# Second item's queries turned by DMA transposes, last item's values loaded in two halves at two times

## The chip, the cores and the metric

The kernel runs on one core of a Trainium2 chip. The metric is the device time of one execution in microseconds (us). A core has five engines that work at the same time, each through its own instructions in order: TensorE (PE in the profile, with its weight loads as PEld), VectorE (DVE), ScalarE (ACT), GpSimd (POOL) and SyncE (SP). Data moves between memory and the core's own buffers by DMA: the transfers that POOL issues run through one software queue (q0 in the profile), those that SP issues through one hardware queue (q1). An engine waits for another, or for a DMA, by a semaphore, and whatever stands behind a waiting instruction on the same engine waits with it.

## What is computed

```python
# B=4 items, H=8 heads, S=768 tokens, D=64; 8 blocks of 96 tokens
P = sinkhorn(sort_net)                     # 5 rounds of exp and row/column division
k_sorted = einsum('bhij,bhjcd->bhicd', P, k_blocks)
v_sorted = einsum('bhij,bhjcd->bhicd', P, v_blocks)
attn = softmax(q_block @ k_sorted_block.T / 8)     # inside each block
x = (attn @ v_sorted_block)                # 3072 tokens x 512
h1 = x @ w1; h2 = x @ w2
out = maximum(h1, h2) @ w_out              # fp32, 3072 x 512
```

## The kernel before

**Stages.** The four batch items are numbered 0 to 3. For each item the kernel sorts keys (`sort_k`, three groups of 32 small matmuls, called KS here), sorts values (`sort_v*`, VS), makes scores and exponentials (`scores`, eight units SC[0] to SC[7], the exponential on ACT), multiplies by values (`values`, VA[0] to VA[7]: eight matmuls into `o_ps`, then on DVE a reciprocal `rs` and a scaled copy `x`), and transposes the result (`x_transposes`, TR[0] to TR[3], into `xT`). Then the dense part follows: `moe_h` makes `max(h1, h2)` as relu((w1-w2)x) plus w2 x, whose second half goes through a product `wc` of w2 and w_out (`w_product`); `moe_out` multiplies by w_out and `wc` and writes the rows out.

**Order.** The order of instructions is written by hand. The first item is the list `front`. After it a loop runs over the items: the dense work of item b is cut into units (for b=0: units 0 to 7 are empty, 8 to 11 are the four `w_product`, 12 to 23 are halves of `moe_out`; for the others units 0 to 7 are `moe_h` and 8 to 19 halves of `moe_out`), and behind unit n stand the steps of the attention of item b+1 that `first_tail`, `second_tail` and `third_tail` list under n. So TensorE always has dense work between the attention steps. An even and an odd `ti` of `moe_out` share one tile `out_ps`; its copy to `o` stands behind the second half of the odd one, that is behind units 15, 19 and 23 of the first item and 11, 15 and 19 of the later ones. A greedy rule (`pick`) shares such copies between ACT and DVE by estimated load.

**Buffers the change touches.** `v_raw` holds raw values of two items side by side: rows 64 to 127 for item 1 and rows 0 to 63 for item 2. `TURN[0]` to `TURN[3]` (`turn_v` on DVE, L250, 24 of 96 columns each, all rows) rearrange it into `v_dc`, whose strided columns are the weights of VS. A VS needs all four turns. Then item 3's values are loaded twice, into both row halves, so that `sort_v_halved` can work from both. When those are turned, `v_raw` is free again and takes item 3's raw keys (columns of TURN[0] and TURN[1]) and raw queries (columns of TURN[2] and TURN[3]). `q_raw` has one buffer; item 2's queries go into the space of `w2_sb`. `q_pair` has one buffer.

**Queries.** `q_transposes(b, half)` makes half of `qT`. For items 0 and 1 it is 24 TensorE transposes into `tq_ps` (L433) and a copy on DVE; for items 2 and 3 `pair_q` first puts the two heads of a pair side by side (`q_pair`, DVE, L407) and SP issues one DMA transpose per half (L419). SC[0], SC[1], SC[4] and SC[5] read half 0, the other four half 1.

**Loads.** POOL issues all loads, in program order: after the weights, item 1's keys, item 1's queries, four pieces of values (items 1 and 2), item 2's keys, item 2's queries; from `first_tail` the four pieces of item 3's values; from `second_tail` item 3's keys and queries.

Of the kernel before, what the change touches and what calls it, by code (L numbers as in the profile page):

```python
# [11 lines left out]
BF16 = mybir.dt.bfloat16  # L12
# [4 lines left out]
def kernel(  # L17
# [16 lines left out]
    nc = tc.nc  # L34
# [12 lines left out]
    R = S // 128  # L47
    PB = 128 // NB
    HP = H // 2
# [5 lines left out]
    const = ctx.enter_context(tc.tile_pool(name="const", bufs=1))  # L55
# [60 lines left out]
    q_raw, qT = {}, {}  # L116
# [15 lines left out]
    def load_q(b, by_pair=False):  # L132
        if b == 2:
            t = w2_sb.rearrange("p t f -> p (t f)")[:, 0 : H * R * D].rearrange(
                "p (h x) -> p h x", h=H
            )
        elif b == 3:
            t = v_raw[:, HB * D :].rearrange("p (h x) -> p h x", h=H)
        else:
            t = qpool.tile([128, H, R * D], BF16, tag="q_raw", name="q_raw", bufs=1)  # L140
        src = q[b].rearrange("h (p r) d -> p h (r d)", r=R)
        for hs in [slice(hp, H, HP) for hp in range(HP)] if by_pair else [slice(0, H)]:
            nc.gpsimd.dma_start(out=t[:, hs], in_=src[:, hs])
        q_raw[b] = t

    k_raw = {}
    v_raw = big.tile([128, BLK * D], BF16, tag="v_raw", name="v_raw")
    k_src = k.rearrange("b h (j ch c) d -> b (h j ch) (c d)", j=NB, ch=2)
    v_src = v.rearrange("b h (j c) d -> b (h j) (c d)", j=NB)
    NCH = 3  # L150

    def load_k(b):
        k_raw[b] = (
            kpool.tile([128, HB * D], BF16, tag="k_raw", name="k_raw")
            if b < 3
            else v_raw[:, 0 : HB * D]
        )
        n = HB * D // NCH
        for ci in range(NCH):
            nc.gpsimd.dma_start(  # L160
                out=k_raw[b][:, ci * n : (ci + 1) * n],
                in_=k_src[b, :, ci * n : (ci + 1) * n],
            )

    def load_v(b, pieces=2, which=None, half=None):
        r0 = (b % 2 if half is None else half) * 64
        n = BLK * D // pieces
        for m in range(pieces) if which is None else [which]:
            nc.gpsimd.dma_start(  # L169
                out=v_raw[r0 : r0 + 64, m * n : (m + 1) * n],  # L170
                in_=v_src[b, :, m * n : (m + 1) * n],
            )
# [30 lines left out]
    def selections(b, eng=nc.gpsimd):  # L203
# [8 lines left out]
        if b == 0:  # L212
# [185 lines left out]
    nc.vector.memset(v_sb[:, :, D : D + 1], 1.0)  # L398
    xT = big.tile([128, 2, 2, 2, 2, TCH], BF16, tag="xT", name="xT")

    q_pair = {}

    def pair_q(b, two):

        if two == 0:
            q_pair[b] = qpool.tile([128, HP, R, 2 * D], BF16, tag="q_pair", name="q_pair", bufs=1)
        nc.vector.tensor_copy(  # L407
            out=q_pair[b][:, :, :, two * D : (two + 1) * D],
            in_=q_raw[b][:, two * HP : (two + 1) * HP].rearrange("p h (r d) -> p h r d", r=R),
        )  # L410
        load["D"] += 900

    def q_transposes(b, half, eng=None):

        if half == 0:
            qT[b] = qpool.tile([128, HP, R, 128], BF16, tag="qT", name="qT")
        if b > 1:
            hps = slice(half * 2, half * 2 + 2)
            nc.sync.dma_start_transpose(  # L419
                out=qT[b][:, hps].rearrange("p h r c -> p (h r) c"),  # L420
                in_=q_pair[b][:, hps].rearrange("p h r d -> p (h r d)"),
            )
            return
        ps = ps_bf16("tq_ps")
        if b == 0 and half == 0:
            nc.tensor.matmul(
                ps[:, 0:128], fill[:, 0:128], ident, is_transpose=True, start=True, stop=True
            )
        for n in range(2 * R):
            hp, r = half * 2 + n // R, n % R  # L430
            c = slice(n * 128, (n + 1) * 128)
            for h2 in range(2):
                nc.tensor.matmul(  # L433
                    ps[h2 * 64 : h2 * 64 + 64, c],
                    q_raw[b][:, hp + 4 * h2, r * D : (r + 1) * D],
                    ident,
                    is_transpose=True,
                    start=True,
                    stop=True,
                )  # L440
# [326 lines left out]
    turn_v(first, "A", 36, 56)  # L767
    turn_v(first, "A", 56, 80)
    block_diagonals_first()
    seen = const.tile([128, 2, 2], BF16, tag="seen", name="seen")  # L770
# [19 lines left out]
    def front_step(step):  # L790

        eng = step[-1] if step[-1] in "AD" else None
        name = step[:-1] if eng else step
        kind = name.rstrip("0123456789ab")
        n = [int(x) for x in name if x.isdigit()]
        if kind == "F":
            fills[0] = 512
        elif kind == "k":
            sort_k(0, n[0], 640 if step == front[0] else 0, eng)
        elif kind == "v":  # L800
            sort_v(0, n[0], 0, eng)
        elif kind == "tq":
            q_transposes(0, n[0], eng)
        elif kind == "SC":
            scores(0, n[0], fills_due())
        elif kind == "VA":
            values(0, n[0], fills_due())
        elif kind == "tx":
            x_transposes(0, n[0], eng)
        elif kind == "tw":  # L810
            w2_transposes(n[0], eng)()
        elif kind == "diff":
            w_difference(n[0])
# [15 lines left out]
    load_w(wo_sb, moe_w_out)  # L829
    w_difference(0, nc.gpsimd)  # L830
    w_difference(1, nc.gpsimd)
    load_k(1)
    for step in front[1:-26]:
        front_step(step)

    load_q(1)
    for piece in range(2):
        for b in (1, 2):
            load_v(b, which=piece)
    load_k(2)  # L840

    for step in front[-26:]:
        front_step(step)
    load_q(2)
    load.update(A=600.0, D=300.0)

    def turn(rows, c0):
# [3 lines left out]
    def sorts_and_scores(b):  # L851
# [2 lines left out]

    SC, VA, TR, KS = sorts_and_scores(1)
    VS = [lambda t=t: sort_v_pair(2, t) for t in range(8)]
    TQ = [lambda half=half: q_transposes(1, half) for half in range(2)]
# [40 lines left out]
    SC, VA, TR, KS = sorts_and_scores(3)  # L898
    third_tail = {
        0: [lambda: q_transposes(3, 0), lambda: q_transposes(3, 1)],  # L900
        2: KS,
        5: SC[0:2],
        6: [VA[0]],
        7: [VA[1], TR[0]],
        8: SC[2:5],
        9: [VA[2]],
        10: [VA[3], TR[1]],
        11: [VA[4]],
        12: SC[5:8],
        13: [VA[5], TR[2]],  # L910
        14: [VA[6]],
        16: [VA[7], TR[3]],
    }
    tails = [first_tail, second_tail, third_tail, {}]
    for b in range(B):
# [52 lines left out]
```

The softmax here doesn't subtract the row's maximum and nothing guards it: scores larger than these inputs give would overflow.

## Time and profile before

| what | value |
|---|---|
| time, median of 13 runs | 166.41 us (166.02 to 167.34) |
| the profiled execution's own time | 167.34 us |
| its span, first to last instruction | 165.5 us |
| granted TensorE clock | 1.000 |
| instructions | 4561 |
| software queue q0: packets, MB written | 11040, 13.37 |
| hardware queue q1: packets, MB | 19200, 10.17 |
| end of the front (start of item 1's KS) | 39.09 us |
| start of item 1's dense part | 71.79 us |
| start of item 2's dense part | 104.83 us |
| start of item 3's dense part | 136.47 us |

The profile is one execution. Its times count from the span's start; the time of the run has 1.8 us more, which lie outside the span. The loads read fp32 and write bf16, so the bytes that the profile gives for q0 are half of those read. "Landing" is the time from a DMA's issue to its last byte.

### The profile page before, as it was taken

Reading aid. Unit: us, or ns where it says so; the run is one execution under the profiler, and the core shown is the slowest. Engines: PE = TensorE matmul, PEld = TensorE weight load, DVE = VectorE, ACT = ScalarE, POOL = GpSimd, SP = SyncE. Lnnn points to the kernel's source line nnn. Section 1 sums busy time; section 2 is a strip of 40 time slices with the busy share of each in tenths; the row PEclk is TensorE's granted clock in tenths of the full one; section 3 lists DMA queues with packets and bytes.
Section 4 is the critical chain, followed back from the end, with each engine's and each line's share of the span. In section 5 each row is a group of like instructions: output and inputs, shape, how many; then the busy total and the mean of one; then the engine's idle time right before and its main releaser. Section 6 shows DMA issues by size and latency. Waiting matters only on the chain.

```text
span 165.5 us, 4561 instructions
## 1 busy us (share of the span) xinstructions
PE 158.1 (96%) x2007; PEld 96.7 (58%) x2025; DVE 77.3 (47%) x170; ACT 82.3 (50%) x101; POOL 33.4 (20%) x61
## 2 busy tenths in 40 slices
PE   7999997999999999999999999999999999999992
PEld 7959775666545555557655554575655546554451
DVE  5868994766276473535278764250642420000011
ACT  3588775816339847046751353467447306642020
POOL 7957987231206000000014020000000000000000
DMA  3999999999999999679525999991025294000333
GB/s 53 197 204 194 162 193 205 209 205 220 210 202 204 218 223 161 178 84 224 115 12 103 181 191 215 196 228 28 0 52 174 50 163 142 0 0 0 131 127 127
DMA packets 30404, 23.90 MB, mean 144 GB/s; under 512 B 16752, under 2 KB 25200, under 8 KB 30384
## 3 DMA queue, kind: packets, MB, share of 16 engines
q0 software_dynamic: 11040, 13.37, 48.6%
q1 hardware_dynamic: 19200, 10.17, 27.9%
q8 instruction: 16, 0.26, 0.7%
q10 hardware_dynamic: 144, 0.07, 0.1%
q14 instruction: 4, 0.03, 0.0%
HBM read 26.75 MB, written 6.29 MB: 200 GB/s over the span
## 4 chain that ended last, share of the span: by engine, by line
PE 87%; DMA 6%; ACT 2%; POOL 2%; issue 1%; DVE 0%
PE out_ps L704 37%; PE h_ps L677 25%; PE fill_ps L82 6%; DMA w_sb<-in_moe_w_dram 6%; PE wc_ps L657 4%; PE o_ps L575 4%; PE k_ps L458 3%; PE s_ps L548 3%; ACT e L556 1%; POOL w_sb L189 1%; PE v_ps L523 1%; PE tq_ps L433 1%; PE tw_ps L638 1%; PE v_ps L500 1%; ACT kT L108 1%
## 5 line engine op out<-in xcount | busy, mean ns | idle before, releaser
L704 PE MATMUL out_ps<-wo_sb,g 128*128 128x512 bf16 (+2 forms) x187 | 46.0, 370 | 1.4 <-issue 1.0
L677 PE MATMUL h_ps<-xT,w_sb 128*128 128x384 bf16 x256 | 44.5, 326 | 0.0
L677 PEld LDWEIGHTS <-w_sb 128*128 128x128 bf16 x256 | 24.0, 98 | 15.5
L556 ACT ACTIVATE e<-s_ps 96x768 bf16<-96x768 f32 x32 | 24.0, 807 | 14.8 <-PE s_ps L548 14.8
L691 ACT ACTIVATE g<-h_ps 128x768 bf16<-128x768 f32 x27 | 21.7, 812 | 17.2 <-PE h_ps L677 17.1
L704 PEld LDWEIGHTS <-g 128*128 128x128 bf16 x200 | 17.1, 97 | 15.8
L704 PE MATMUL out_ps<-wc,xT 128*128 128x512 bf16 (+2 forms) x98 | 24.7, 370 | 0.1
L108 ACT COPY o<-out_ps 128x1024 f32<-128x1024 f32 x10 | 10.1, 1013 | 28.0 <-PE out_ps L704 25.2
L592 DVE TENSOR_TENSOR x<-o_ps,rs 96x512 bf16<-96x512 f32 x32 | 22.0, 686 | 1.1
L704 PEld LDWEIGHTS <-xT 128*128 128x128 bf16 x100 | 9.6, 97 | 11.2
L575 PEld LDWEIGHTS <-e 96*128 96x128 bf16 x256 | 11.7, 97 | 5.8 <-DVE v_sb L110 0.2
L586 DVE RECIPROCAL rs<-o_ps 96x8 f32<-96x8 f32 x32 | 6.4, 199 | 17.9 <-PE o_ps L575 17.9
L739 DVE COPY o<-out_ps 128x512 f32<-128x512 f32 (+1 forms) x2 | 1.2, 625 | 27.6 <-PE out_ps L704 27.6
L575 PE MATMUL o_ps<-v_sb,e 96*128 96x65 bf16 x256 | 12.7, 193 | 0.0
L110 DVE CAST kT<-k_ps 128x1024 bf16<-128x1024 f32 x6 | 7.2, 1222 | 9.5 <-PE k_ps L458 9.5
L110 DVE CAST v_sb<-v_ps 96x1024 bf16<-96x1024 f32 x7 | 8.5, 1218 | 5.1 <-PE v_ps L523 2.2
L160 POOL DMA_DIRECT2D v_raw<-in_k_dram x3 | 2.5, 838 | 35.1 <-DVE v_dc L250 31.4
L108 ACT CAST v_sb<-v_ps 96x1024 bf16<-96x1024 f32 x9 | 8.8, 1017 | 1.5 <-PE v_ps L500 0.8
L82 PEld LDWEIGHTS <-fill 128*128 128x128 bf16 x98 | 8.1, 130 | 1.5 <-DVE fill L73 1.2
L169 POOL DMA_DIRECT2D v_raw<-in_v_dram x11 | 6.3, 579 | 12.8 <-DMA v_raw<-in_v_dram 5.6
L82 PE MATMUL fill_ps<-fill 128*128 128x118 bf16 x92 | 7.8, 274 | 1.2 <-DVE fill L73 1.2
L693 DVE TENSOR_SCALAR g<-h_ps 128x768 bf16<-128x768 f32 x5 | 4.8, 957 | 8.7 <-PE h_ps L677 8.6
(97 smaller groups left out, 145.3 us busy)
## 6 DMA issues: line engine op xcount, KB each, us to landing
out_dram<-o SPq DMA_DIRECT2D x11, 512.0 KB, 3.0
v_raw<-in_v_dram POOLq DMA_DIRECT2D x8, 384.0 KB, 13.8
k_raw<-in_k_dram POOLq DMA_DIRECT2D x9, 256.0 KB, 11.0
w_sb<-in_moe_w_dram POOLq DMA_DIRECT2D x4, 256.0 KB, 5.9
w_sb<-in_moe_w_dram POOLq DMA_DIRECT2D x2, 512.0 KB, 10.3
wo_sb<-in_moe_w_out_dram POOLq DMA_DIRECT2D x2, 512.0 KB, 13.9
v_raw<-in_v_dram POOLq DMA_DIRECT2D x3, 256.0 KB, 4.6
q_raw<-in_q_dram POOLq DMA_DIRECT2D x4, 192.0 KB, 8.8
```

The lines of the kernel that those rows point to most:

```text
L82: nc.tensor.matmul(ps[:, 0:w], w0, fill[:, 0:w], start=True, stop=True)
L108: nc.scalar.copy(out=out_ap, in_=in_ap)
L110: nc.vector.tensor_copy(out=out_ap, in_=in_ap)
L169: nc.gpsimd.dma_start(out=v_raw[r0 : r0 + 64, m * n : (m + 1) * n], in_=v_src[b, :, m * n : (m + 1) * n],)
L556: nc.scalar.activation(out=e[:, 0 : 8 * BLK].rearrange("p (t c r) -> p t c r", t=8, r=R), in_=ps[0:BLK] .rearrange("p (t f) -> p t f", t=8 ...
L575: nc.tensor.matmul(ps[:, h2 * 512 + ii * 65 : h2 * 512 + (ii + 1) * 65], e[:, (h2 * 4 + ii) * BLK : (h2 * 4 + ii) * BLK + 128], v_sb[:, m0 ...
L586: nc.vector.reciprocal(out=rs, in_=ov[:, :, :, 64])
L592: nc.vector.tensor_tensor(out=x, in0=ov[:, :, :, 0:D], in1=rs.to_broadcast([BLK, 2, 4, D]), op=ALU.mult,)
L657: nc.tensor.matmul(ps[:, 0:512], w2T[:, fb, dmt * 128 : (dmt + 1) * 128], wo_sb[:, fb, :], start=(fb == 0), stop=(fb == NFB - 1),)
L677: nc.tensor.matmul(h_ps[ch, t][:, m * 512 : m * 512 + TCH], w1_sb[:, hp, fb * 128 : (fb + 1) * 128], xT[:, b % 2, ch, hp % 2, hp // 2, :], ...
L691: nc.scalar.activation(out=g, in_=src, func=AF.Relu)
L704: nc.tensor.matmul(dst, g_tiles[b, ch, m // 2][:, m % 2, off : off + 128] if m < NFB else xT[:, b % 2, ch, hp % 2, hp // 2, off : off + 12 ...
```

## The change

Item 1's queries are transposed by DMA, as items 2 and 3 are. Their load moves ahead of the keys'. A new `hold_loads` puts a POOL copy of four bytes out of `qT` in front of the following loads: POOL waits there until that half of `qT` is complete. The values of items 1 and 2 are loaded in eight pieces behind this hold, then item 2's queries, then its keys. Item 3's values are loaded one row half at a time: half 0 behind unit 15 of the first item, half 1 behind unit 1 of the second and behind a hold on item 2's `qT`. Their two pieces take alternate runs of 512 elements. Item 3's queries are loaded ahead of its keys. In the three tails most steps stand later by one to four units (SC[4] and SC[5] stand earlier); `pair_q` and the transposes of items 2 and 3 now stand at units 0 and 1 of the tails that use them. In `second_tail` the turns are taken in the order 2, 3, 0, 1.

```diff
@@ load_v
-            nc.gpsimd.dma_start(
-                out=v_raw[r0 : r0 + 64, m * n : (m + 1) * n],
-                in_=v_src[b, :, m * n : (m + 1) * n],
-            )
+            if half is None:
+                c = slice(m * n, (m + 1) * n)
+                dst, src = v_raw[r0 : r0 + 64, c], v_src[b, :, c]
+            else:
+                dst, src = (
+                    x.rearrange("p (k two x) -> p two k x", two=2, x=512)[:, m]
+                    for x in (v_raw[r0 : r0 + 64], v_src[b])
+                )
+            nc.gpsimd.dma_start(out=dst, in_=src)
@@
+    def hold_loads(b, hp=HP - 1):
+
+        nc.gpsimd.tensor_copy(out=seen[:, 0], in_=qT[b][:, hp, R - 1, 126:128])
@@ q_transposes
-        if b > 1:
+        if b > 0:
@@ loads behind the front's start
-    load_k(1)
     for step in front[1:-26]:
         front_step(step)
     load_q(1)
-    for piece in range(2):
-        for b in (1, 2):
-            load_v(b, which=piece)
-    load_k(2)
+    load_k(1)
     for step in front[-26:]:
         front_step(step)
+    for half in range(2):
+        pair_q(1, half)
+    for half in range(2):
+        q_transposes(1, half)
+    hold_loads(1, 1)
+    for piece in range(4):
+        for b in (1, 2):
+            load_v(b, 4, which=piece)
     load_q(2)
+    load_k(2)
@@ first_tail
-        7: KS,
-        9: [TQ[0], TURN[0]],
-        10: [SC[0], TQ[1], TURN[1]],
-        11: SC[1:4] + TURN[2:4] + [lambda half=half: load_v(3, half=half) for half in range(2)],
-        12: VS[0:3],
-        13: VS[3:6],
-        14: VS[6:8] + [SC[4]],
-        15: [VA[0], lambda: pair_q(2, 0)],
-        16: [VA[1], lambda: pair_q(2, 1)],
-        17: SC[5:8] + [TR[0]],
-        18: [VA[2]],
-        19: [VA[3], TR[1]],
-        20: [VA[4]],
-        21: [VA[5], TR[2]],
-        22: [VA[6], VA[7], TR[3]],
+        9: KS,
+        10: SC[0:2],
+        11: SC[4:6],
+        12: SC[2:4] + [TURN[0]],
+        13: SC[6:8] + [TURN[1]],
+        14: [TURN[2]],
+        15: [TURN[3], lambda: load_v(3, half=0)],
+        16: VS[0:2],
+        17: VS[2:5],
+        18: VS[5:8],
+        19: [VA[0]],
+        20: [VA[1], TR[0], VA[2]],
+        21: [VA[3], TR[1]],
+        22: [VA[4], VA[5], TR[2]],
+        23: [VA[6], VA[7], TR[3]],
@@ second_tail
-        0: [lambda: q_transposes(2, 0), lambda: q_transposes(2, 1)],
+        0: [lambda: pair_q(2, 0), lambda: pair_q(2, 1)],
+        1: [
+            lambda: q_transposes(2, 0),
+            lambda: q_transposes(2, 1),
+            lambda: hold_loads(2),
+            lambda: load_v(3, half=1),
+        ],
         2: KS,
-        4: SC[0:2],
-        5: [VA[0]],
-        6: SC[2:4] + [TURN[0]],
-        7: [VA[1], TR[0]],
-        8: [VA[2], TURN[1]],
-        9: [VA[3], TR[1], TURN[2]],
-        10: SC[4:7],
-        11: [VA[4], TURN[3]],
-        12: [VA[5], TR[2], lambda: load_k(3), lambda: load_q(3)],
-        13: [VA[6]],
+        5: SC[0:2],
+        6: [VA[0]],
+        7: SC[2:4],
+        8: [VA[1], TR[0]],
+        9: [VA[2]],
+        10: SC[4:7] + [TURN[2]],
+        11: [VA[3], TR[1], TURN[3], lambda: load_q(3)],
+        12: [VA[4], TURN[0]],
+        13: [VA[5], TR[2], TURN[1], lambda: load_k(3)],
         14: SC[7:8] + VS[0:2],
-        15: [VA[7], TR[3]],
+        15: [VA[6]],
         16: VS[2:4],
-        17: [lambda: pair_q(3, 0)],
-        18: [lambda: pair_q(3, 1)],
+        17: [VA[7], TR[3]],
@@ third_tail (its other steps, from SC on, one unit later)
-        0: [lambda: q_transposes(3, 0), lambda: q_transposes(3, 1)],
+        0: [lambda: pair_q(3, 0), lambda: pair_q(3, 1)],
+        1: [lambda: q_transposes(3, 0), lambda: q_transposes(3, 1)],
```

More of the change, by code (lines that the diff above doesn't have):

```diff
@@ L399 @@
     xT = big.tile([128, 2, 2, 2, 2, TCH], BF16, tag="xT", name="xT")
+    seen = const.tile([128, 2, 2], BF16, tag="seen", name="seen")
     q_pair = {}
+    def hold_loads(b, hp=HP - 1):
+        nc.gpsimd.tensor_copy(out=seen[:, 0], in_=qT[b][:, hp, R - 1, 126:128])
     def pair_q(b, two):
@@ L769 @@
     block_diagonals_first()
-    seen = const.tile([128, 2, 2], BF16, tag="seen", name="seen")
     nc.gpsimd.tensor_copy(out=seen[0:G, 0], in_=p_bf[:, NB - 1, NB - 2 :])
@@ L856 @@
     VS = [lambda t=t: sort_v_pair(2, t) for t in range(8)]
-    TQ = [lambda half=half: q_transposes(1, half) for half in range(2)]
     TURN = [lambda c=c: turn(both, c) for c in (0, 24, 48, 72)]
     first_tail = {
-        7: KS,
-        9: [TQ[0], TURN[0]],
-        10: [SC[0], TQ[1], TURN[1]],
-        11: SC[1:4] + TURN[2:4] + [lambda half=half: load_v(3, half=half) for half in range(2)],
-        12: VS[0:3],
-        13: VS[3:6],
-        14: VS[6:8] + [SC[4]],
-        15: [VA[0], lambda: pair_q(2, 0)],
-        16: [VA[1], lambda: pair_q(2, 1)],
-        17: SC[5:8] + [TR[0]],
-        18: [VA[2]],
-        19: [VA[3], TR[1]],
-        20: [VA[4]],
-        21: [VA[5], TR[2]],
-        22: [VA[6], VA[7], TR[3]],
+        9: KS,
[13 more added lines that the diff above has]
+        23: [VA[6], VA[7], TR[3]],
     }
@@ L899 @@
     third_tail = {
-        0: [lambda: q_transposes(3, 0), lambda: q_transposes(3, 1)],
+        0: [lambda: pair_q(3, 0), lambda: pair_q(3, 1)],
+        1: [lambda: q_transposes(3, 0), lambda: q_transposes(3, 1)],
         2: KS,
[L902 to L912, printed above, removed]
+        6: SC[0:2],
+        7: [VA[0]],
+        8: [VA[1], TR[0]],
+        9: SC[2:5],
+        10: [VA[2]],
+        11: [VA[3], TR[1]],
+        12: [VA[4]],
+        13: SC[5:8],
+        14: [VA[5], TR[2]],
+        15: [VA[6]],
+        17: [VA[7], TR[3]],
     }
```

## The prediction

> **What bounds the kernel now.** I read the shares of busy time first, then the chain of waits by engine.
>
> ```profile
> PE 158.1 (96%) x2007; PEld 96.7 (58%) x2025; DVE 77.3 (47%) x170; ACT 82.3 (50%) x101; POOL 33.4 (20%) x61
> ...
> PE 87%; DMA 6%; ACT 2%; POOL 2%; issue 1%; DVE 0%
> ```
>
> TensorE is busy for 96% and the chain lies on it for 87%. So taking work off TensorE pays in full, and any wait of TensorE costs in full, unless it falls into one of its few gaps. Next I read the chain in order of time where item 1's queries are turned:
>
> ```profile
> 44.28 0.79 PE tq_ps L433 x24
> ...
> 47.18 0.79 PE tq_ps L433 x24
> ...
> 49.84 0.47 ACT wc L108
> 50.31 0.02 issue
> 50.32 2.22 ACT e L556 x3
> ```
>
> The reader sees two blocks of 24 transposes on the path, 0.79 us each, and a stretch where three exponentials of one burst stand on it. In the windows of this stage TensorE is busy 31.88 of 32.70 us between 39.10 and 71.80; in 51.90 to 56.50, right behind that burst, it is idle for 0.40 us.
>
> **What goes: 1.6 + 0.4 us.** 2 x 0.79 = 1.58 us of transposes leave TensorE. Two DVE copies of 0.958 us (the qT row of L110) leave and two of 0.55 us (q_pair, L407) come, on a DVE that waits 1.83 us for the first of them now: nothing either way. Scores come in four pairs instead of bursts of three, so I count the 0.40 us gap as gone. Sum: -2.0 us.
>
> **What takes its place: a chain of DMA and DVE work up to item 1's values.** By the DMA answers for single issues, where the last number is the time to landing:
>
> ```profile
> k_raw<-in_k_dram POOLq DMA_DIRECT2D x1, 256.0 KB, 10.3
> ...
> q_raw<-in_q_dram POOLq DMA_DIRECT2D x1, 768.0 KB, 16.3
> ...
> qT<-q_pair SPq DMA_TRANSPOSE x1, 4.8
> ```
>
> The first keys' piece was issued at 25.01 and landed at 35.3; the others follow 1.2 us apart, and the queries (issued at 26.65) at 42.95, some 5.2 us after the last piece. With queries first I expect them 5.2 us after 34.1 (35.3 - 1.2), at 39.3, and the keys at 42.9. KS now stands behind two `w_product` blocks (3.56 us from 40.72 to 44.28 in the chain), at 42.65, with its last group at 43.7: covered by 0.8 us. DVE's last front work ends at 38.5, so pair_q runs from 39.35 to 40.45. SP's queue is empty until 59.83, so the first transpose goes out at 40.45, 4.8 us alone (the issue at 74.61), the second 2 us behind. But the keys still flow until 42.9. The xT transposes show what that does: 2.8 us to landing with q0 quiet (119), 5.5 at 61.5, and 8.5 at 95.8 beside a load:
>
> ```profile
> xT<-x SPq DMA_TRANSPOSE x1, 8.5
> ```
>
> So the first half of qT lands between 45.2 (alone) and 49 (8.5 us). I take 46.1, because only half of its time lies beside the keys. SC[0] is due at 46.06, so it is covered by nothing: each later microsecond is lost on TensorE. Half 1 (48) is first wanted at 50.1.
>
> **The hold.** POOL waits for half 0 of qT. Behind it on POOL stand all loads that are left: eight pieces of values, item 2's queries and keys. Before, the values were issued from 27.54 to 34.58 and landed at 44.6 to 49.9, so q0 never ran dry; now it stands empty from 42.9 to about 47. From a release at 46.1: 0.2 us for the copy, 3.5 us to the first landing (estimate: a 256 KB piece landed in 3.9 us on the quiet queue at 84.8, this one has 192 KB), then seven more at 0.9 us (the pieces of twice the size came 1.7 to 1.9 us apart): 56.1. TURN[3] (0.83 us) ends at 57.0. TensorE reaches VS at 56.2: from SC[0] two pairs of scores before unit 12 (0.9), one `w_product` (1.8), units 12 to 16 (1.30 each, six matmuls of 0.216), two more pairs (0.9). **Wait 0.8 us**, nothing if qT lands at 45.2, up to 3.7 if at 49.
>
> [...]
>
> **Item 1's end.** VA[0] to VA[7] now fill units 19 to 23, two a unit. DVE needs 0.84 us a VA (94.78 to 95.61 in the last fence below: 0.83) and also makes the second `o` (1.22, by the order of its instructions). With V for VS's start: o until V+7.6, VA[0] 8.4, VA[1] 9.25, VA[2] 10.1, VA[3] 10.95. TR[1] is then issued, and lands 2.8 to 3.7 us later (V+13.8 to 14.7; 5.5 or more if the first half of item 3's values still loads, which I put at 57 to 68). Item 1's dense part comes at V+13.4 and its third matmul (0.33 us on) needs TR[1]. **Wait 0.7 us** (0 to 2.5). Before, TR[1] stood four units ahead of this point.
>
> **Item 2's tail: DVE gets the turns in one lump.** The timeline of DVE and PE around item 3's values:
>
> ```profile
> 92.05 1.22 DVE L110 COPY o<-out_ps 128x1024 f32<-128x1024 f32 x1 [1.68 <-ACT e L556]
> ...
> 94.03 0.83 DVE L250 COPY v_dc<-v_raw 128x768 uint32<-128x768 uint32 x1
> 94.78 0.19 DVE L586 RECIPROCAL rs<-o_ps 96x8 f32<-96x8 f32 x1
> ...
> 95.61 0.19 DVE L586 RECIPROCAL rs<-o_ps 96x8 f32<-96x8 f32 x1
> ...
> 95.84 0.69 DVE L592 TENSOR_TENSOR x<-o_ps,rs 96x512 bf16<-96x512 f32 x1
> ...
> 96.69 0.63 PE L500 MATMUL v_ps<-bd,v_dc 64*128 64x64 bf16 x32
> ```
>
> From 92.05 DVE works without a gap: o, VA, one turn, VA, VA, done at 96.53. TensorE comes to VS at 96.69. In the changed order the same stretch has o, VA[3], TURN[3], VA[4], TURN[0], VA[5], TURN[1]: two turns more, each 0.75 us from start to start (94.03 to 94.78). 96.53 + 1.5 = 98.05, and now VS needs the last of them, where before TURN[3] was done at 94.86. TensorE's own way from unit 11 to VS has the same units and as many VAs. **Wait 1.4 us**, the surest term here: it needs no DMA. Its load is in time: half 1 of the values goes out after qT of item 2 (about 8.5 us into the part) and lands by 15.5; TURN[2] wants it at 17.8. Item 3's queries then go out at about 23 and keys at 26 of that part, and land by about 32 and 35; KS of item 3 wants the keys at 38. That is covered by 3 us, and the queries' new place costs nothing.
>
> Moving pair_q and the transposes of items 2 and 3 to units 0 and 1 costs nothing: before they waited on SP behind `out_dram` (73.34, then 74.61), SC stands a unit later, 9.4 us into the part, and qT needs 7.
>
> **Sum.** -1.6 - 0.4 + 0.8 + 0.7 + 1.4 = +0.9 us. The profiled execution goes from 167.34 to 168.2. It stands 0.93 above the median of the runs; I put the same step on the median, 166.41: **167.3 us**. A change under 0.2% (0.33 us) can't be told from none.
>
> **Rivals.**
> (a) *Slightly slower*, the sum above: 166.8 to 168.2. Chance 0.50.
> (b) *The DMA waits do not come* (qT in 4.8 us, values as quick as 45.2 gives, TR[1] in 2.8): -2.0 + 1.4 = -0.6, 165.8. For it: the quiet q0. Against it: four links with no slack. If DVE also catches up, because `o` or a VA comes earlier, up to -2.0, 164.4. Chance 0.24, with the second 0.05 of it.
> (c) *The turning of qT is late for good*: the keys' flow costs 8.5 us as at 95.8, or the queries land no sooner than before (42.95). [...] by the 8.5 us row it lands at 49. Then -2.0 + 3.7 + 1.0 + 1.4 = +4 us at most; 169.3 in the middle. Chance 0.20.
> (d) *No change*: the first two waits sum to 0.6 instead of 1.5, 166.4. Chance 0.06. The hold may also do little of what it says, since the three keys' loads are issued ahead of it: that is part of (c).
>
> With the edges of (a) and (b) reaching into the middle band: faster 0.23, same 0.14, slower 0.63. The range leaves out the far ends of (b) and (c): 165.4 to 169.2; case (a) alone 166.8 to 168.2.
>
> **What would show it.** PE busy down by about 1.6 us. About 1.4 us of idle TensorE ahead of item 3's value sort, ended by DVE `v_dc`; that is the step I hold surest. A wait of VS for item 1 on `v_dc` near 57, a wait of `h_ps` on DMA `xT` near 71, DMA bytes near zero around 43 to 47. If item 1's dense part starts near 69.7, (b) is right; at 73 or later, (c). If PE does not wait before item 3's VS, my DVE chain is wrong.

## The result and the profile after

| | time, median (lowest to highest), runs | ratio to before, 95% interval |
|---|---|---|
| before | 166.30 us (165.63 to 167.47), 48 | |
| after | 168.62 us (167.78 to 169.75), 11 | 1.0137 (1.0113 to 1.0162) |

Medians count every run; the ratios leave out runs more than 1.5% above the fastest of their kernel (three of six in e1 and in e2, one each in e9, e10 and e11).

The changed kernel is 2.3 us slower; the forecast was 0.9 us slower (167.3, range 165.4 to 169.2). The direction held, the size did not. The profiled execution is the slowest of the eleven, 169.75 us (span 167.9, granted clock 1.000), as the one of before was near the top of its own runs. That matters below: two of the waits differ from execution to execution.

The page of the changed kernel, busy shares and the chain by engine:

```profile
PE 156.3 (93%) x1959; PEld 94.1 (56%) x1977; DVE 76.7 (46%) x170; ACT 82.7 (49%) x101; POOL 37.4 (22%) x67
...
PE 61%; DMA 17%; DVE 10%; POOL 4%; issue 3%; ACT 3%; DVEq 0%; POOLq 0%
```

TensorE works 1.8 us less (158.1 before), yet the chain that ended last lies on it for 61% instead of 87%: DMA went from 6% to 17% and DVE from nothing to 10%. Which waits these are, the view of waits of the changed kernel tells (engine, line, cause: us in total, times, longest):

```profile
PE v_ps L533 <- DVE v_dc L255: 1.3, 1, 1.3
...
PE v_ps L510 <- DVE v_dc L255: 1.2, 1, 1.2
...
PE h_ps L687 <- DVE x L602: 0.8, 1, 0.8
PE h_ps L687 <- DMA xT<-x: 0.3, 1, 0.3
```

None of these rows stands among the waits of before. They are item 1's value sort (L533), item 3's value sort (L510) and the start of item 1's dense part (L687). By stages, from the starts of instructions in the timelines of both traces (the dense part's start is taken from its third product, 0.33 us after the first where nothing waits; the four times in the first table are from the chain, which counts a product only from the end of the one before, 0.1 to 0.2 us later):

| stage | before | after | difference | forecast |
|---|---|---|---|---|
| the front | 39.0 | 38.4 | -0.6 | 0 |
| front's end to start of item 1's dense part | 32.6 | 33.9 | +1.3 | -0.5 |
| to start of item 2's dense part | 33.0 | 34.4 | +1.3 | +1.4 |
| to start of item 3's dense part | 31.65 | 31.65 | 0 | 0 |
| to the last copy (L737, now L747) | 26.2 | 26.2 | 0 | 0 |
| from there to the end of the program | 3.0 | 3.4 | +0.4 | 0 |

The front is the same work in both, in the changed kernel up to its first `w_product`; its end differs among the traces of the changed kernel and its variants from 37.4 to 39.3.

The chain of the changed kernel in order of time (start, us, what) from item 1's queries to its value sort:

```profile
38.95 4.69 DMA qT<-q_pair
...
43.76 0.18 POOL seen L411
...
44.21 2.55 POOL v_raw L177 x5
...
47.78 8.45 DMA v_raw<-in_v_dram
...
56.32 0.83 DVE v_dc L255
...
57.19 0.64 PE v_ps L533 x32
```

This is the hold at work: transpose, POOL's release, the issue of eight pieces, the last of which lands 8.45 us after its issue, then the turn, then TensorE. The transpose itself took 4.69 us and was in time. The pieces landed 3.5 to 12.0 us (the last, at 56.2) after the first of them was issued at 44.21: 1.2 us apart, not 0.9 as in the forecast.

The start of item 1's dense part, in the timeline of TensorE (start, us, what, and in brackets the idle time before it), first before, then after; then TR[0] and TR[1] after in the answers on single DMA issues, whose last number is the time to landing:

```profile
71.63 1.30 PE L677 MATMUL h_ps<-xT,w_sb 128*128 128x384 bf16 x7
...
71.91 0.48 PE L687 MATMUL h_ps<-xT,w_sb 128*128 128x384 bf16 x2 [0.81 <-DVE x L602]
72.65 1.14 PE L687 MATMUL h_ps<-xT,w_sb 128*128 128x384 bf16 x6 [0.25 <-DMA xT<-x]
```

```profile
xT<-x SPq DMA_TRANSPOSE x1, 5.0
...
xT<-x SPq DMA_TRANSPOSE x1, 4.1
```

TR[0] was issued at 66.73 and landed at 71.78, TR[1] at 68.52 and at 72.60. The two gaps of TensorE end within 0.2 us of these landings. The row blames DVE for the first gap, but the first products read what TR[0] writes, and experiments 1, 5 and 9 to 11 decide for the DMA.

The chain of the changed kernel ahead of item 3's value sort:

```profile
92.46 1.23 DVE o L110
...
94.43 0.83 DVE v_dc L255
...
96.10 0.73 DVE v_dc L255
...
97.66 0.74 DVE v_dc L255
...
98.44 0.64 PE v_ps L510 x32
```

DVE works from `o` to the third turn without a gap (the rows left out are the copies of VA[3] to VA[5]), and TensorE follows 0.04 us behind. That is the forecast's VectorE chain, link by link.

### The profile page after: what moved, and what is told of

Same layout as the page of the kernel before. It is cut to its first block, busy times and chain, and to the rows that moved or that the text cites. A ratio compares the mean times of both kernels' runs of the same rounds, so it can differ in the third digit from the quotient of the medians.

```text
span 167.9 us, 4477 instructions
## 1 busy us (share of the span) xinstructions
PE 156.3 (93%) x1959; PEld 94.1 (56%) x1977; DVE 76.7 (46%) x170; ACT 82.7 (49%) x101; POOL 37.4 (22%) x67
## 4 chain that ended last, share of the span: by engine, by line
PE 61%; DMA 17%; DVE 10%; POOL 4%; issue 3%; ACT 3%; DVEq 0%; POOLq 0%
PE out_ps L714 28%; PE h_ps L687 23%; DMA w_sb<-in_moe_w_dram 5%; DMA v_raw<-in_v_dram 5%; PE o_ps L585 3%; DMA qT<-q_pair 3%; DMA xT<-x 2%; PE k_ps L468 2%; POOL v_raw L177 2%; DVE v_dc L255 2%; PE s_ps L558 2%; POOL w_sb L194 1%; PE v_ps L533 1%; DVE x L602 1%; DMA p_sb<-in_sort_net_dram 1%
## 5 line engine op out<-in xcount | busy, mean ns | idle before, releaser
L687 PE MATMUL h_ps<-xT,w_sb 128*128 128x384 bf16 x256 | 44.3, 326 | 1.1 <-DVE x L602 0.8
L687 PEld LDWEIGHTS <-w_sb 128*128 128x128 bf16 x256 | 24.1, 98 | 16.7 <-DVE x L602 0.9
L701 ACT ACTIVATE g<-h_ps 128x768 bf16<-128x768 f32 x28 | 22.5, 812 | 18.8 <-PE h_ps L687 18.6
L108 ACT COPY o<-out_ps 128x1024 f32<-128x1024 f32 x9 | 9.1, 1013 | 27.3 <-PE out_ps L714 26.3
L255 DVE COPY v_dc<-v_raw 128x768 uint32<-128x768 uint32 (+1 forms) x9 | 7.2, 801 | 7.6 <-DMA v_raw<-in_v_dram 7.6
L177 POOL DMA_DIRECT2D v_raw<-in_v_dram x15 | 8.5, 592 | 5.6 <-DVE v_dc L255 4.3
L558 PEld LDWEIGHTS <-kT 64*128 64x128 bf16 x256 | 6.0, 94 | 5.1 <-issue 3.7
L558 PE MATMUL s_ps<-qT,kT 64*128 64x96 bf16 x256 | 8.5, 204 | 0.2 <-DVE qT L110 0.2
## 6 DMA issues: line engine op xcount, KB each, us to landing
w_sb<-in_moe_w_dram POOLq DMA_DIRECT2D x2, 512.0 KB, 10.1
```

The costliest lines, as they stand in the source:

```text
L108: nc.scalar.copy(out=out_ap, in_=in_ap)
L177: nc.gpsimd.dma_start(out=dst, in_=src)
L255: nc.vector.tensor_copy(out=dst.bitcast(U32).rearrange("p (d c) -> p d c", c=BLK)[:, :, c0:c1], in_=src.bitcast(U32).rearrange("p (c d) -> ...
L558: nc.tensor.matmul(ps[:, h2 * 512 + ii * 128 : h2 * 512 + ii * 128 + BLK], kT[b][rows, (hp * 8 + i) * BLK : (hp * 8 + i) * BLK + 128], rhs ...
L687: nc.tensor.matmul(h_ps[ch, t][:, m * 512 : m * 512 + TCH], w1_sb[:, hp, fb * 128 : (fb + 1) * 128], xT[:, b % 2, ch, hp % 2, hp // 2, :], ...
L701: nc.scalar.activation(out=g, in_=src, func=AF.Relu)
```

## Experiments

Each kernel is the changed one with the edit shown. Ratios are to the kernel before, with 95% intervals; the changed kernel itself stands at 1.0137.

### Is turning by DMA worth its price, and what do the holds do?

**1. Item 1's queries back on TensorE (e8).** No hold on item 1; the rest of the change stays.

```diff
-        if b > 0:
+        if b > 1:
@@
-    for half in range(2):
-        pair_q(1, half)
-    for half in range(2):
-        q_transposes(1, half)
-    hold_loads(1, 1)
@@
+    TQ = [lambda half=half: q_transposes(1, half) for half in range(2)]
@@ first_tail
-        9: KS,
-        10: SC[0:2],
+        9: KS + [TQ[0]],
+        10: SC[0:2] + [TQ[1]],
```

> The changed kernel with item 1's queries turned on TensorE again and no first hold; loads in the changed order, tails as changed, the two blocks of 24 transposes behind KS and SC[1]. Theory (the DMA turning saves 1.6 us of TensorE and costs 1.8 us of waiting for the values): TensorE works 1.6 us more, VS does not wait, the rest stays or gains up to 0.7 us since item 3's first half loads earlier: 167.7 to 168.5, near 168.6. Rival (the DMA turning is a gain and the later waits alone make the change slower): 169.8 to 170.3.

168.04 us, ratio 1.010 (1.007 to 1.013). Its interval overlaps that of the changed kernel: 1.6 us less work on TensorE gave no time that can be told from none; the median is even 0.6 us lower with the turning on TensorE. Values came early, so neither item 1's value sort nor its dense part waits; the first stage takes 32.85 us, nearly as before, and the loss of item 2's part stays whole (34.5 us). Of the four rows of waits this kernel keeps the one of item 3's value sort, 1.2 us, and TR[0] and TR[1] are quick:

```profile
xT<-x SPq DMA_TRANSPOSE x1, 2.9
...
xT<-x SPq DMA_TRANSPOSE x1, 2.8
```

The load of item 3's first half started 5.8 us earlier here (51.67 instead of 57.43) and was in at 61.8, before TR[0] went out at 66.83.

**2. No hold on item 1's queries (e1).** `hold_loads(1, 1)` is taken out, so the values go out at once.

> The changed kernel without the hold on item 1's qT; the eight value pieces go out from about 27 us on. Theory (the hold makes the values late): the wait of item 1's value sort on v_dc (1.8 us in the changed kernel) goes, qT's first half lands beside the loads at 5.5 to 8.5 us instead of 4.7, so SC[0] waits 0 to 2 us; item 2's loads come earlier, so the transposes of x meet a quiet queue and the wait at the start of item 1's dense part (1.4 us) shrinks. Time 166 to 167.5, against 168.6. Rival (the hold earns its keep): qT lands at 50 or later, TensorE waits 4 us or more for it, time 170 or more.

185.99 us, ratio 1.1063 (1.1002 to 1.1124). The forecast priced a transpose beside a load at 8.5 us at most. Half 0, issued at 38.35, took 16.9 us; half 1 is on this kernel's chain:

```profile
45.40 19.09 DMA qT<-q_pair
```

and the windows (stretch, its length, busy time and number of instructions of PE, PEld, DVE, ACT and POOL, then the granted clock, the DMA share, GB/s) show TensorE without work and then at half its clock:

```profile
44.88:47.78 2.90, 0.00 (x0) 0.00 (x0) 2.86 (x4) 0.00 (x0) 0.18 (x1) 1.00 1.15 196
47.78:50.00 2.22, 0.00 (x0) 0.00 (x0) 0.81 (x1) 0.00 (x0) 0.38 (x1) 0.50 1.32 170
55.39:61.44 6.05, 6.05 (x43) 2.69 (x44) 0.00 (x0) 3.17 (x5) 0.00 (x0) 0.50 1.25 177
```

So the hold costs a wait of about a microsecond (1.3 us at item 1's value sort) and saves 17 (168.62 against 185.99 us). A second loss rides on the first: TensorE stopped at 44.88, its granted clock was 0.50 from 47.78 on, 2.9 us later, and the first 6 us of the work that followed, from 55.39, ran at 0.50 too.

**3. The same, values in short runs (e12).** To see whether the size of the load's packets bears on the transpose's time, the four pieces of an item take alternate runs of 512 elements, so that the load's packets are smaller.

```diff
+            if pieces == 4:
+                dst, src = (
+                    x.rearrange("p (k four x) -> p four k x", four=4, x=512)[:, m]
+                    for x in (v_raw[r0 : r0 + 64], v_src[b])
+                )
@@
-    hold_loads(1, 1)
```

> The kernel without the first hold, but with the values of items 1 and 2 in alternate runs of 512 elements (1 KB packets on the written side instead of 3 KB). Theory [...]: half 0 of qT lands 8 to 11 us after its issue instead of 16.9 and half 1 follows in the same measure until the queries of item 2 go through; time 176 to 181 against 186. Rival (a transpose simply waits until the other queue has run dry): 17 to 19 us to landing as before, time 184 to 188.

184.96 us, ratio 1.1116 (1.1067 to 1.1165). Half 0 took 14.2 us instead of 16.9, and half 1 landed at 64.9 (64.5 without the short runs), so the theory missed. The packets say more. Here are those of the two queues in stretches of three traces: e1 and e12 from 43 to 46 us, and the changed kernel from 42 to 44, where only the transposes run (packets, MB, share of the engines' time):

```profile
q0 software_dynamic: 232, 0.57, 95.6%
q1 hardware_dynamic: 232, 0.06, 13.7%
...
q0 software_dynamic: 487, 0.46, 91.0%
q1 hardware_dynamic: 482, 0.12, 31.2%
...
q1 hardware_dynamic: 1918, 0.48, 129.0%
```

In e1 and e12 the counts of the two queues are equal to 1%, 232 and 232 beside the long packets, 487 and 482 beside the short ones. The transpose's packets, of 256 bytes, went at 77 a microsecond beside the values' packets of 3,072 bytes, at 161 beside those of 1,024 bytes and at 959 alone. So the size counts, and half 0 still gained less than the theory had, for two reasons. In both kernels no packet of half 0 moved in the first 3.9 us after its issue (1.2 us in the changed kernel). And in e1 the last packet of the values started at 47.8; behind them came item 2's queries, whose packets have 768 bytes in both kernels; beside them 187 packets a microsecond passed (49 to 52 us). An estimate for e12 from these numbers is 3.9 us and 1,536 packets at 161 a microsecond, 13.4 us.

**4. Item 3's values in one go, turns spread (e2).** Both halves go out behind unit 15 of the first item, without the second hold, so the turns can stand where DVE has time.

```diff
-        15: [TURN[3], lambda: load_v(3, half=0)],
+        15: [TURN[3]] + [lambda half=half: load_v(3, half=half) for half in range(2)],
@@ second_tail: hold_loads(2) and load_v(3, half=1) leave unit 1
+        7: SC[2:4] + [TURN[2]],
+        8: [VA[1], TR[0], TURN[3]],
+        9: [VA[2], TURN[0]],
+        10: SC[4:7],
+        11: [VA[3], TR[1], TURN[1], lambda: load_q(3)],
```

> The changed kernel with both halves of item 3's values loaded at unit 15 of the first tail (no hold on item 2's qT) and the turns spread over units 7, 8, 9 and 11 of the second. Theory (four turns in a lump make VectorE late): TensorE's wait of 1.3 us ahead of item 3's value sort goes, item 2's part takes 33.1 us instead of 34.5, time 167.2 to 167.5. The longer load at 57 to 73 us may cost the transposes of x at the start of item 1's dense part up to 1 us more. Rival (TensorE waits there for something else, such as item 3's late data): item 2's part stays at 34.5.

179.53 us, ratio 1.068 (1.0621 to 1.0739): a clear miss. TensorE's wait:

```profile
PE h_ps L687 <- DMA xT<-x: 7.8, 2, 5.8
```

The four pieces keep the software queue full when TR[0] is issued at 66.98, and the transpose takes 10.06 us. Loading the second half late is what spares item 1's dense part a wait of 5.8 us; the other 1.9 us stand at the start of item 2's.

**5. Both halves late (e5).** `load_v(3, half=0)` moves behind the hold on item 2's queries, so that nothing loads beside TR[0] and TR[1].

> The changed kernel with half 0 of item 3's values moved behind the hold on item 2's qT, beside half 1. Theory (the x transposes of item 1's end are slow because that half is loading): TR[1] lands 2.8 to 3.0 us after its issue instead of 4.1, the wait at the start of item 1's dense part falls from 1.4 to about 0.9 us (what is left is VectorE's scaled copies). Paid back later: both halves land at about 92 instead of 88, TURN[2] starts 2 to 3 us late and the wait ahead of item 3's value sort grows from 1.3 to 3 or 4. Time 169.5 to 171. Rival (the load does not matter there): TR[1] still takes 4 us.

173.06 us, ratio 1.04 (1.0359 to 1.044), worse than was expected. But it shows what it was made for: TR[0] landed after 3.5 us, TR[1] after 2.8, and item 1's dense part followed its last VA without a wait, with DVE's order of work unchanged. The time came back later, on the chain of this kernel: the last piece of both halves, issued at 83.27, was in at 93.9 only, and item 2's part takes 40.0 us instead of 34.4.

### The wait for item 1's values

**6. Two pieces instead of four (e6).**

```diff
-    for piece in range(4):
+    for piece in range(2):
         for b in (1, 2):
-            load_v(b, 4, which=piece)
+            load_v(b, which=piece)
```

> The changed kernel with the values of items 1 and 2 in two pieces each, as before the change, behind the same hold. Theory (small pieces on an empty queue come 1.2 us apart instead of 0.9): the last piece lands 1 to 2 us earlier, the wait of VS falls from 1.8 to about 0.5, time 167.5 to 168. Rival (the rate after a hold is set by the queue's start and by the neighbours, not by the piece): the last piece lands at the same time within 0.5 us, and the turns, which then start only with the large pieces, end no earlier: time 168.5 to 169.5.

167.88 us, ratio 1.0102 (1.0067 to 1.0137); not told apart from the changed kernel. The time lies where the theory put it, but not for its reason: from the release to the end of the last turn it is 13.6 us, and 13.4 with four pieces. The size of the pieces made no difference here.

**7. An earlier release (e7).** POOL waits for `q_pair` instead of `qT`, then works 2.74 us on scratch and issues the values.

```diff
-    hold_loads(1, 1)
+    idle = const.tile([128, HP, 384], BF16, tag="idle", name="idle")
+    nc.gpsimd.tensor_copy(out=seen[:, 0], in_=q_pair[1][:, HP - 1, R - 1, 126:128])
+    nc.gpsimd.tensor_tensor(
+        out=idle, in0=w1_sb[:, :, 0:384], in1=w1_sb[:, :, 0:384], op=ALU.subtract
+    )
```

> The changed kernel with another hold: POOL waits for q_pair instead of qT and then works 3.2 us on a scratch tile, so that the values go out at about 42.4 instead of 44.2, before the first half of qT has landed. Theory (VS waits for the values, and they for the release): VS starts up to 1.8 us earlier, its wait goes, time 166.8 to 167.3. The second half of qT then has loads beside it, but SC needs it only at 49.5. Rival (a transpose with loads beside it starves until they are through, as without the hold): qT's second half lands at 52 or later, TensorE waits 3 us or more at SC[2], time 170 or more.

167.46 us, ratio 1.0061 (1.0032 to 1.009): 1.2 us less than the changed kernel. The values go out at 40.90, and the chain passes the value sort on TensorE alone:

```profile
50.90 3.99 PE out_ps L714 x18
54.89 0.57 PE v_ps L533 x32
```

The wait ahead of the dense part stays (1.3 us late). Half 1 of `qT` took 6.2 us instead of 4.1. That is far from e1's 19.1 us: here the transpose was mostly through when the load began, its last packet of data started at 43.95, the load's first at 43.76.

### The turns of item 3

**8. One `o` of item 1 on ScalarE (e4).** The copy at the head of the DVE chain, 1.23 us, leaves DVE.

```diff
-            evac(o.rearrange("p t n -> p (t n)"), ps, 1024)
+            evac(
+                o.rearrange("p t n -> p (t n)"), ps, 1024, eng="A" if (b, ti) in ((1, 1),) else None
+            )
```

> The changed kernel with one copy moved: item 1's first output copy (o, 1.22 us, behind unit 11) on ScalarE. Theory (the VectorE chain o, 3 VAs, 3 turns ends 1.3 us after TensorE comes to item 3's value sort): the chain is 1.2 us shorter, the wait falls from 1.3 to at most 0.2 us, time 167.2 to 167.5. Rival (the wait is for the data of item 3 or for a buffer): item 2's part stays at 34.5 us, time 168.6.

167.63 us, ratio 1.0082 (1.0059 to 1.0104), 1.0 us less; item 2's part takes 33.4 us instead of 34.4. TensorE's timeline ahead of this value sort:

```profile
95.75 0.64 PE L510 MATMUL v_ps<-bd,v_dc 64*128 64x64 bf16 x32 [0.26 <-DVE v_dc L255]
```

The wait is 0.26 us, and 1.2 in the changed kernel. The DVE chain set this stage.

### The start of item 1's dense part

**9. One `o` of item 0 on ScalarE (e3).** The forecast's reason for this wait was DVE: `o` delays the VAs, these delay TR[1]. The edit is that of e4 with `((0, 3),)`.

> The changed kernel with one copy moved: item 0's second output copy (o, 1.22 us, behind unit 19) on ScalarE instead of VectorE. Theory (VectorE's backlog of o and eight VAs makes TR[1] late): x for TR[1] and its transpose come 1.0 to 1.2 us earlier, the wait of 1.4 us at the start of item 1's dense part falls to 0.2 to 0.5, time 167.4 to 167.8. Rival (the transpose is late because item 3's values are loading): it lands at 72.6 whatever VectorE does, time within 0.3 us of 168.6.

168.45 us, ratio 1.0137 (1.0092 to 1.0183): no change. **10. The same, and the VAs and TRs a unit earlier (e9)** gave 168.61 us, ratio 1.0124 (1.0083 to 1.0165), no change either.

```diff
-        19: [VA[0]],
-        20: [VA[1], TR[0], VA[2]],
-        21: [VA[3], TR[1]],
-        22: [VA[4], VA[5], TR[2]],
+        19: VA[0:2],
+        20: [TR[0]] + VA[2:4] + [TR[1]],
+        21: [VA[4]],
+        22: [VA[5], TR[2]],
```

> The changed kernel with VA[0] to VA[3] at units 19 and 20 (two each) and TR[0], TR[1] at unit 20, item 0's second output copy on ScalarE as in the kernel that moved it alone. Theory (the wait of 1.4 us at the start of item 1's dense part is TR[1] issued 11.3 us behind the start of VS): TR[1] goes out about 1 us earlier, the wait falls to 0.3 to 0.5 us, time 167.4 to 167.9 against 168.6. Rival (the transpose only takes as much longer, since the load beside it runs until 69): time within 0.3 us of 168.5.

**11. Products that need only TR[0] first (e13).** The first two tiles of item 1's `moe_h` take the products of TR[0]'s half, then those of TR[1]'s.

```diff
+        if b == 1:
+
+            def two(hps):
+                for t in range(2):
+                    if hps[0] == 0:
+                        moe_h_products(1, 0, t, hps)
+                    else:
+                        moe_h(1, 0, t, "A", hps)
+
+            units[0:2] = [lambda: two((0, 2)), lambda: two((1, 3))]
```

> The changed kernel with the first two units of item 1's dense part in another order: of both tiles first the products that need TR[0] alone (8 matmuls, 1.3 us), then the others. Theory (1.4 us of waiting there, 1.0 until VectorE frees a buffer at 71.9, then 0.4 more until TR[1] has landed): only the second part is covered, 168.1 to 168.4. Rival (TR[1] is the whole wait): 167.3 to 167.7.

168.46 us, ratio 1.0122 (1.0076 to 1.0168): no gain. TensorE now waits once, for TR[0], issued at 67.41; the row blames DVE again, but the gap ends 0.1 us after TR[0]'s landing at 72.6 (5.2 us in the DMA answer):

```profile
72.72 1.30 PE L687 MATMUL h_ps<-xT,w_sb 128*128 128x384 bf16 x7 [0.94 <-DVE rs L596]
```

What the traces share is in the next table. "Left" is how long the load of item 3's first half still ran when TR[0] was issued, "late" by how much the third product came later than 0.37 us behind the start of the last VA product (0.04 to the first product and 0.33 on to the third).

| kernel | left at TR[0]'s issue | TR[0] | TR[1] | late |
|---|---|---|---|---|
| after | 3.5 | 5.0 | 4.1 | 1.4 |
| e7 | 3.4 | 5.0 | 4.0 | 1.3 |
| e3 | 3.1 | 4.7 | 3.1 | 0.9 |
| e4 | 2.7 | 4.7 | 3.1 | 0.85 |
| e6 | 1.5 | 3.9 | 3.0 | 0.3 |
| e5 | no load | 3.5 | 2.8 | 0.1 |
| e8 | over for 5.1 | 2.9 | 2.8 | 0.1 |

In the five rows where they meet, TR[0] lands 1.6 to 2.4 us after the load's end, and it takes longer the more of the load is left. In the traces of e10, e11 and e13 to e16 the second is less regular: 2.4 to 4.5 us were left, and TR[0] took 5.1 to 5.7 (5.2 in e13, where 2.4 were left). DVE still makes `o` in e5, e6 and e8, and they are hardly late. In e8 the copy `x` ahead of the dense part even stands as far behind the VA products as in the changed kernel (71.23 after 70.55; 71.13 after 70.45), and TensorE goes on at 71.03, before that copy has begun. The load decides.

How it does so is shown only in part. On SP's queue the store of item 0's second `o` stands ahead of TR[0], issued 1.3 to 2.0 us before it. In the five rows that store lands 0.7 to 0.8 us before TR[0] (71.10 and 71.78 in the changed kernel). So the load may hold up the store, and TR[0] behind it; no run moved the store.

The table also shows the scatter: the edit of e4 works after this point, and the same schedule is late by 0.85 in its execution and by 1.4 in that of the changed kernel.

### Put together

**12. Release and item 1's `o` (e10 = e7 and e4).**

> The earlier release and the copy o of item 1 on ScalarE together. Theory (two waits at different places, each on TensorE's path, so that the gains add: 1.2 and 1.0 us): 166.2 to 166.7, level with the kernel before (166.3). Rival (the earlier start only lets item 3's values or the DMA queue become the limit): 167 or more.

166.89 us, ratio 1.0029 (1.0007 to 1.0051). This is 1.7 us less than the changed kernel, of the 1.2 and 1.0 that the two edits give alone: most of both gains adds up, to just short of the kernel before.

**13. All three (e11 = e10, item 0's `o` on ScalarE and the units of e9).**

> The earlier release, both copies o on ScalarE and VA[0] to VA[3] a unit earlier: the three waits on TensorE named in the explanation all taken away. Theory: 1.2 + 1.0 + 0.7 to 1.0 off 168.6, so 165.4 to 166.0, faster than the kernel before by the 1.6 us of transposes less what is left of the waits. Rival (the waits aren't the whole loss): 166.3 or more.

166.36 us, ratio 1.0005 (0.9981 to 1.0029): level. TR[0] went out at 63.83, 2.9 us earlier than in the changed kernel, but the load ended as much earlier (67.3 instead of 70.2). TR[0] took 5.3 us and again landed behind the load, at 69.2.

**14 to 16. Three tries on top of e11.** e14 adds the order of products of e13, e15 moves item 3's value sort to units 15 and 17, e16 does both.

> The kernel with all three waits treated, and the products in the order of e13. Theory (TR[1] lands 0.5 us after TensorE has done what needs TR[0] alone): 165.8 to 166.0. Rival (buffers): 166.3.

> The kernel with all three waits treated, and item 3's value sort one unit later (15 and 17). Theory (TensorE still waits 0.3 to 0.5 us there for the last turn): item 2's part falls from 33.60 to 33.1 to 33.3 us, time 165.9 to 166.1. Rival (the rest lies in the burst of scores): 33.6 stays.

> e14 and e15 in one. Theory (the gains add): 165.3 to 165.7, faster than the kernel before by 0.4 to 0.6%. Rival: 166.0 or more.

166.46, 166.65 and 166.57 us; ratios 1.0009 (0.9989 to 1.0028), 1.0014 (0.9996 to 1.0032) and 1.0005 (0.9983 to 1.0026). None is faster. In e15 item 2's part takes 33.6 us, no less than with e4's edit alone (33.4): the value sort comes later by as much as it no longer waits. No version was found that beats the kernel before.

## Why the forecast was right in direction and short in size

Three steps of the sum failed. It took a gap of 0.40 us for idle time that would go; it put nothing for the end of the program; and it put the two waits that hang on DMAs too low, one of them for a wrong reason. They are 0.6, 0.4 and 0.5 us of the miss; the turns of item 3 give 0.1 back.

**What leaves TensorE: right, 1.6 us** (busy time fell by 1.8). **The gap of 0.40 us: wrong, and misread.** The first stage can be added up in several traces: before's 32.6 less 1.58, plus the wait of item 1's value sort, plus what "late" has.

| kernel | value sort waits | late | sum | measured |
|---|---|---|---|---|
| after | 1.3 | 1.4 | 33.7 | 33.9 |
| e3 | 0.4 | 0.9 | 32.4 | 32.6 |
| e4 | 0.6 | 0.85 | 32.5 | 32.7 |
| e6 | 0.7 | 0.3 | 32.0 | 32.2 |
| e5 | 1.0 | 0.1 | 32.1 | 32.3 |
| e7 | 0 | 1.3 | 32.3 | 32.5 |

Each time 0.2 us more are measured, where the forecast had 0.4 less. This step, "I count the 0.40 us gap as gone", is 0.6 us of the miss. Most of that gap was no idle time. In the window that the forecast read, 51.90 to 56.50 of before, it is 0.08 us ahead of a value sort and these two:

```profile
53.15 0.38 PE L704 MATMUL out_ps<-wo_sb,g 128*128 128x512 bf16 x1 [0.16 <-issue]
53.37 1.03 PE L704 MATMUL out_ps<-wc,xT 128*128 128x512 bf16 x4
...
55.36 1.24 PE L704 MATMUL out_ps<-wo_sb,g 128*128 128x512 bf16 x5 [0.16 <-issue]
```

Each is a unit of six products with five recorded: the first record is missing from the trace, and part of its time reads as idle. In the whole stage before's trace has 67 products of `out_ps`; e6 and e8 have all 72, and no such gap. So there was little to gain. And a new wait came: in all six traces TensorE waits 0.14 to 0.15 us ahead of VA[0], in the changed kernel until 63.80, 0.04 us after ACT's copy of the sorted values. What makes up the rest of the 0.2 us no run separates.

**qT beside the last keys: right that no wait came, by a wide margin.** With queries ahead of keys the queries landed at 37.4 (forecast 39.3), and half 0 of `qT` after 4.7 us at 43.6 (forecast 46.1). Its first packet started at 40.2 and the keys' last at 40.7, so the two hardly met, and rival (c) was not put to the test.

**The hold: right in mechanism, 0.8 us forecast, 0.4 to 1.3 measured.** Here luck helped, as two errors nearly cancelled: the release came 2.3 us earlier than forecast (43.8, not 46.1), the pieces 1.2 us apart instead of 0.9; TensorE also came to the value sort earlier. e7 removes the wait and 1.2 us of time.

**Start of the dense part: right wait, wrong reason, 0.7 us forecast, 0.85 and 1.4 measured** (e4's trace, in which this stage is unchanged, and the changed kernel's). The forecast put it on DVE's `o` and gave the transpose 2.8 to 3.7 us, with "5.5 or more if the first half of item 3's values still loads" as an end that it did not take. That end is what happened (5.0 and 4.1). e3 and e9 take DVE's `o` away and gain no time; e5 and e8 take the load away and the wait with it. Most of the wait is for TR[0] (0.8 us in the changed kernel), not for TR[1]. Its own numbers had the load at 57 to 68 and TR[0] inside that span, so the end was the case to take.

**The turns in one lump: right.** 1.4 us forecast; 1.3 measured in the changed kernel and 1.4 in e8; e4 gets 0.9 of it back in the stage named, 1.0 of the time. (The forecast's 96.53 + 1.5 is 98.03, not 98.05, which changes nothing.)

**Not in the sum: 0.4 us at the end, which are no work.** The last store lands 2.0 us after the last copy before and 2.1 in the changed kernel (164.51 and 166.60). At the end of the program SP waits for the DMAs' semaphores in nine steps, one behind the other. These are the steps that were left when the last store had landed, before and after:

```profile
L963 SPq EVENT_SEMAPHORE  x2: 27/28/28, 164.5 to 164.6; - x2
...
L981 SPq EVENT_SEMAPHORE  x8: 28/28/28, 166.6 to 167.0; - x8
```

The step that waits for the last store is the eighth of the nine before and in e8, where SP issues 30 DMAs, and the second after and in all other variants, where it issues 32: that store has another semaphore. Six more steps, 0.06 us apart, are 0.4 us.

So at the median the miss of 1.4 us (2.3 against 0.9) divides into 0.6 for the gap, 0.4 for the end, -0.1 for the turns and, by what is left, 0.5 for the two waits together: 2.0 instead of 1.5, between the 1.45 of e4's trace and the 2.7 of the changed kernel's. That last part takes the front as equally long in both, which one trace of before can't settle.

**The price of rivals.** The forecast weighed a transpose beside a load at 8.5 us. With a queue full throughout, e1 measured 16.9 and 19.1 us and e2 10.1; in e1 the transpose moved 77 packets a microsecond beside the long ones, and 959 on a quiet queue (experiment 3). The change is not worse than 2.3 us because its two holds keep the queue empty at the right times: without the first the kernel takes 17.4 us more (e1), with the second half of item 3's values not held back 10.9 (e2). Turning by DMA with its hold gains nothing over turning on TensorE (e8).

## What to carry to other kernels

Work taken off the bounding engine and given to DMA needed a quiet queue beside it here (168.62 us with the hold, 185.99 without). The hold that makes the queue quiet delayed all loads behind it, and item 1's value sort waited 0.4 to 1.3 us for them, so price the hold with the load's restart (3.5 us to the first landing), not the transpose alone. Before steps are put together ahead of a matmul, add up the other engine's queue from its last free moment: this one sum, made from one timeline, was right to 0.1 us. And where a transfer's landing time has two rows, with and without a load beside it (5.0 us in the changed kernel and 2.9 in e8 for TR[0]), look up in the same sums whether the load is still running. Before a gap in a busy engine's timeline is counted as gain, count the instructions beside it: before's trace has 67 of 72 products of `out_ps` in that stage.

## What was not expected of the hardware

- Beside a full software queue a DMA transpose and the load moved equal numbers of packets: 232 and 232 in 3 us of e1, 482 and 487 in e12. Half of `qT` (128 x 1536 bf16, packets of 256 bytes) took 16.9 and 19.1 us to land in e1, and 4.7 on a quiet queue.
- In the changed kernel and the ten variants where the load of item 3's first half was still running when `xT`'s transpose TR[0] was issued (e2 and e9 not counted), TR[0] landed 1.2 to 2.8 us behind the load's end.
- Eight loads of 192 KB after an empty queue landed 1.2 us apart, and four of 384 KB needed the same time in all (13.4 and 13.6 us from release to last turn).
- After 2.9 us without work (44.88 to 47.78) TensorE was granted 0.50 of its clock, and 0.50 still stood over the first 6 us of work that followed (e1, 55.4 to 61.4 us).
- The same program end took 0.4 us more because the last store's semaphore stood earlier in a row of nine waits, second instead of eighth (1.0 us from the last landing to the end before, 1.3 after).
